# The weight sums of a wide pair's quarters on GpSimd instead of VectorE, in a three-layer attention and MoE kernel

## Chip, cores and metric

The kernel runs on one core of one Trainium2 chip. The metric is device microseconds of one execution. Three executions before the change took 1060.55, 1061.58 and 1061.87 us; their median, 1061.58 us, is the time before.

## What is computed

A chunked attention, then two dense layers with different activations, all in float32:

```python
def reference(**kwargs):
    attn_out = _attn_ref(...)              # (4, 8, 768, 64), chunks of 32 queries
    x = attn_out.transpose(0, 2, 1, 3).reshape(B * S, H * D)   # 3072 x 512
    x = _moe_ref(x, w_in, w_out, alpha)    # h = x @ w_in; g = max(h,0) + alpha*min(h,0); g @ w_out
    return _moe2_ref(x, w_in, w_out)       # g = h * tanh(softplus(h)); g @ w_out
```

`w_in` is 512 x 2048 and `w_out` 2048 x 512 in both layers.

## The kernel before

**Numbers and blocks.** Every float32 operand of a matmul is kept as a rounded high part and a low part (its rest), and a product is three matmuls: high by high, high by low, low by high. The 3072 rows are six blocks of 512. A layer's 2048 hidden units are 16 units of 128 (`NJ`), or 8 pairs (`NPAIR`).

**Stages.** Attention is woven into the first blocks of layer 1. Blocks 0 to 3 of layer 1 are done unit by unit (`gemm1` line 1069, `gemm2` line 1118). Blocks 4 and 5 are done together in the *wide stage* (`pair1`, products at line 1552, second matrix at line 1648). Layer 2 follows (lines 1227 and 1359).

**The wide stage.** A pair of units and two blocks make a 2 x 2 by 2 x 2 matrix product. It is done with seven products instead of eight, so it needs sums and differences of the quarters of the weights and of the inputs. `wide_x` makes those of the inputs once. `sums_of_w(p)` makes those of pair p's weights, one pair ahead of `pair1(p)`:

- it first undoes the split: for both units, high plus low part into the tile `tt` (128x512 each, two additions, line 1513);
- then four differences of quarters in place in `tt` (128x256, line 1523), all by VectorE;
- then ScalarE copies `tt` rounded into `to` (line 1524), and VectorE subtracts to get the low half (line 1526).

`tt` has one buffer (in the profile a `b` tile), so the additions of pair p+1 wait for line 1526 of pair p. `to` has two (the tiles `xh` and `xl` of an old ring). Products 3 to 6 of a pair read `to`; products 0 to 2 read the weights themselves.

**A pair's evacuations.** Product 3 starts bank B, product 0 bank A. ScalarE copies both out (line 1559). Then products 4 and 2 add on, product 5 goes to A again, product 6 to A, product 1 to B anew. Between them VectorE adds each bank to what was kept (`more`, line 1562: one operand in PSUM, one in SBUF): `e3` after product 2, `e2` after product 5, `e1` after product 1. Product 6 cannot start before `e2` has been read out of bank A, nor product 1 before `e3` has been read out of bank B. The activation (lines 1566, 1567, 1570) and a split (lines 1629, 1630) make operands for the second matrix. Its matmuls (lines 1118 and 1648, *pieces* of three) stand between the products.

**Other work on VectorE in this stage.** The weights of layer 2 are read, converted and split in background jobs (lines 341, 344, 383, 392), and blocks 2 and 3 end (lines 1082, 1092).

**What sets the order.** The program is written down as tasks (`Plan.add`: engine, planned cost, function, reads, writes). `Plan.run` computes for each task when it is due, from the planned costs backwards, and then walks forward in time, giving each engine the ready task that is due first. The instructions are issued in that order, fixed for each engine, and each engine runs its queue in order. So a planned cost (`d_(512)`, 0.6 us, for a 128x512 VectorE operation) also sets where all other instructions stand. The five engines are VectorE, ScalarE, TensorE, SyncE (which issues the DMAs), and GpSimd, which so far has only memsets, the identity and the sign of `alpha` at the start.

Of the kernel before, what the change touches and what calls it, by code (L numbers as in the profile page):

```python
# [51 lines left out]
class Pool:  # L52
# [5 lines left out]
    def add(self, make, after):  # L58
        self.free.append((make, list(after)))
# [130 lines left out]
def chunked_attention_moe_moe_kernel(  # L190
# [16 lines left out]
    nc = tc.nc  # L207
# [48 lines left out]
    def a_(n):  # L256
        return 0.1 + 0.83e-3 * n

    def d_(n, fast=False):
        return 0.066 + n / (1920.0 if fast else 960.0)  # L260
# [735 lines left out]
    pool, wpool = Pool(), Pool()  # L996
# [510 lines left out]
    def sums_of_w(p):  # L1507
        w = [weights[0, "i", 2 * p + n] for n in range(2)]
        tt, to = second["tt"].next(), wide["t"].next()
        for n in range(2):  # L1510
            add(
                "dve", d_(512),
                lambda n=n: nc.vector.tensor_add(
                    tt.t[:, (1 - n) * 512 : (2 - n) * 512], w[n].t[:, 0, :].bitcast(F32), w[n].t[:, 1, :].bitcast(F32)
                ),
                [w[n]], [(tt, n)],
            )

        def q(i):
            return tt.t[:, PLACE.index(i) * HB :][:, :HB]  # L1520

        for to_, x, y in ((3, 5, 3), (5, 4, 5), (4, 4, 3), (6, 6, 4)):
            add("dve", d_(HB), lambda to_=to_, x=x, y=y: nc.vector.tensor_sub(q(to_), q(x), q(y)), [], [tt])
        add("act", a_(1024), lambda: nc.scalar.copy(to.t[:, :1024], tt.t), [tt], [(to, "h")])
        add(
            "dve", d_(1024), lambda: nc.vector.tensor_sub(to.t[:, 1024:], tt.t, to.t[:, :1024].bitcast(F32)),
            [tt, (to, "h")], [(to, "l")],
        )
        return to
# [177 lines left out]
    for layer, blk, j in tiles:  # L1707
# [13 lines left out]
        n = BLOCKS[blk][1]  # L1721
# [37 lines left out]
    for layer, blk, j in pend:  # L1759
        reload1(j)  # L1760
        parts.extend((6, part) for part in gemm2_parts(layer, blk, j))
    tops = {0: sums_of_w(0)}
    for p in range(NPAIR):
        if p + 1 < NPAIR:
            tops[p + 1] = sums_of_w(p + 1)
        if p in JOBS_AT:
            next(jobs)(plan.now + 25.0)
        ends_ = pair1(p, xs, take)
        take(12)
        if p < NPAIR - 1:  # L1770
            for j in (2 * p + 1, 2 * p):
                parts.extend(wide_parts(WIDE, j, (p, j) == (0, 1), False))
# [108 lines left out]
```

## Time and profile before

| | before |
|---|---|
| median of three executions | 1061.58 us |
| the profiled execution | 1062.53 us |
| its span on the core | 1060.7 us |
| TensorE busy | 1053.6 us (99%) |
| VectorE busy | 769.7 us (73%) |
| ScalarE busy | 605.3 us (57%) |
| GpSimd busy | 6.7 us (1%) |
| mean granted TensorE clock | 0.998 |

The span lies 1.8 us below the execution's own time, which includes what stands around it. Busy shares are means over stages: VectorE's 73% is made of stretches of over 90% and others under 60%. Instructions of one engine overlap a little at their ends, so the time that one takes in a full queue is the distance between two starts, not its duration.

### The profile page before, as it was taken

The numbers are of one execution on the slowest core, as the hardware profiler recorded it, in microseconds if no ns is written. First come the engines' busy times: TensorE is split into PE (matmuls) and PEld (weight loads), VectorE is DVE, ScalarE is ACT, GpSimd is POOL, SyncE is SP. The second block draws the span as 40 slices with busy tenths as digits, with TensorE's granted clock in tenths as the row PEclk, the third lists the DMA queues.
The fourth block names the chain that finished last, engine by engine and source line by source line (L and its number), as shares of the span: only waits on it lengthen the run. The fifth ranks groups of instructions, "written<-read, shape, count | busy, mean of one in ns | idle before, by whom it ended". The sixth has DMA issues, their size and how long they took to land.

```text
span 1060.7 us, 22413 instructions
## 1 busy us (share of the span) xinstructions
PE 1053.6 (99%) x8249; PEld 905.6 (85%) x8249; DVE 769.7 (73%) x1626; ACT 605.3 (57%) x1505; POOL 6.7 (1%) x19
## 2 busy tenths in 40 slices
PE   9999999999999999999999999999999999999998
PEld 5888888888888888888888889999999999999998
DVE  6899487779877799999595246776576875475586
ACT  6888545565556555787585344654444654454453
POOL 2000000000000000000000000000000000000000
PEclk9999999999999999999999999999999999999999
DMA  9968783876577655577799898687888778778786
GB/s 275 301 218 232 258 282 108 236 243 210 198 235 229 213 179 195 169 254 255 242 303 334 283 304 265 218 259 251 263 271 252 227 245 250 229 239 253 229 267 203
DMA packets 136732, 256.68 MB, mean 242 GB/s; under 512 B 13872, under 2 KB 38960, under 8 KB 136624
## 3 DMA queue, kind: packets, MB, share of 16 engines
q1 hardware_dynamic: 136624, 255.26, 75.2%
q8 instruction: 65, 1.06, 0.4%
q14 instruction: 43, 0.35, 0.1%
HBM read 203.56 MB, written 51.64 MB: 241 GB/s over the span
## 4 chain that ended last, share of the span: by engine, by line
PE 99%; issue 0%; DVE 0%; DVEq 0%
PE bank L1359 23%; PE bank L1227 22%; PE bank L1118 17%; PE bank L1069 17%; PE bank L1648 8%; PE bank L1552 7%; PE bank L803 2%; PE bank L737 1%; PE bank L1666 1%; PE bank L681 0%; PE bank L614 0%; PE bank L850 0%; PE bank L874 0%; DVE xh L1420 0%; DVEq L1876 0%
## 5 line engine op out<-in xcount | busy, mean ns | idle before, releaser
L1227 PE MATMUL bank<-wi,wo 128*128 128x512 f32 x672 | 180.7, 392 | 0.0
L1069 PE MATMUL bank<-xh,wi 128*128 128x512 f32 (+1 forms) x528 | 170.9, 386 | 0.0
L1118 PE MATMUL bank<-gh,wo 128*128 128x512 f32 x512 | 170.2, 392 | 0.0
L1227 PEld LDWEIGHTS bank<-wi,wo 128*128 128x128 f32 x672 | 121.5, 189 | 21.3
L1069 PEld LDWEIGHTS bank<-xh,wi 128*128 128x128 f32 x528 | 98.2, 188 | 19.9
L1118 PEld LDWEIGHTS bank<-gh,wo 128*128 128x128 f32 x512 | 96.1, 188 | 20.6
L1069 PE MATMUL bank<-xl,wi 128*128 128x512 f32 (+1 forms) x264 | 101.1, 383 | 0.0
L1118 PE MATMUL bank<-gl,wo 128*128 128x512 f32 x256 | 99.7, 390 | 0.0
L1227 PE MATMUL bank<-wo,wo 128*128 128x512 f32 x336 | 93.0, 393 | 0.0
L1359 PE MATMUL bank<-wo,wi 128*128 128x256 f32 x588 | 80.2, 283 | 0.0
L1359 PEld LDWEIGHTS bank<-wo,wi 128*128 128x128 f32 x588 | 77.1, 191 | 3.0
L1359 PE MATMUL bank<-wo,wo 128*128 128x256 f32 x558 | 76.9, 283 | 0.0
L1359 PEld LDWEIGHTS bank<-wo,wo 128*128 128x128 f32 x558 | 73.7, 191 | 3.1
L1227 PEld LDWEIGHTS bank<-wo,wo 128*128 128x128 f32 x336 | 60.8, 189 | 10.1
L1088 ACT ACTIVATE rstrip<-bank 128x512 f32<-128x512 f32 x64 | 39.0, 609 | 47.1 <-PE bank L1069 45.3
L1081 ACT CAST gh<-rstrip 128x512 fp32r<-128x512 f32 x64 | 40.4, 632 | 44.3 <-PE bank L1118 22.6
L1092 DVE SCALAR_TENSOR_TENSOR rstrip<-rstrip,nalpha 128x512 f32<-128x512 f32 x64 | 47.8, 748 | 22.4 <-ACT rstrip L1089 21.6
L1069 PEld LDWEIGHTS bank<-xl,wi 128*128 128x128 f32 x264 | 49.6, 188 | 9.5
L891 DVE STREAM_TRANSPOSE aT<-s 32x256 f32<-32x256 f32 x128 | 55.8, 436 | 2.4
L1082 DVE TENSOR_TENSOR gl<-rstrip,gh 128x512 fp32r<-128x512 f32 x64 | 44.0, 688 | 18.1 <-ACT gh L1081 17.3
L1118 PEld LDWEIGHTS bank<-gl,wo 128*128 128x128 f32 x256 | 48.1, 188 | 9.7
L756 ACT ACTIVATE s<-bank,su 128x64 f32<-128x64 f32 x160 | 48.7, 351 | 7.5 <-DVE su L773 7.5
(399 smaller groups left out, 1999.3 us busy)
## 6 DMA issues: line engine op xcount, KB each, us to landing
wo<-w2o SPq DMA_DIRECT2D x237, 256.0 KB, 3.4
wo<-w2i SPq DMA_DIRECT2D x168, 256.0 KB, 3.4
wo<-w1o SPq DMA_DIRECT2D x49, 512.0 KB, 4.3
w2o<-wo SPq DMA_DIRECT2D x57, 256.0 KB, 3.1
w2i<-wo SPq DMA_DIRECT2D x56, 256.0 KB, 3.2
wo<-in_w_out_dram SPq DMA_DIRECT2D x24, 512.0 KB, 7.6
wi<-in_w_in_dram SPq DMA_DIRECT2D x16, 512.0 KB, 9.0
w1o<-wo SPq DMA_DIRECT2D x16, 512.0 KB, 5.6
```

The lines of the kernel that those rows point to most:

```text
L756: nc.scalar.activation(s()[:, i, z, g], ps(z)[:, i, g], AF.Exp, bias=st.t[:, 0, n : n + 1], scale=0.125, accum_out=st.t[:, 1, n : n + 1],)
L891: nc.vector.transpose(dst[:, :, m // 2, m % 2], src[:, :, keys])
L1069: nc.tensor.matmul(bk.t[:, lo:hi], a, b, start=kk == 0 and i == 0, stop=kk == KT - 1 and i == 2)
L1081: add("act", a_(n), lambda: nc.scalar.copy(g.t[0], src.t[0]), [src], [(g, "h")], at=at)
L1082: add("dve", d_(n), lambda: nc.vector.tensor_sub(g.t[1], src.t[0], g.t[0].bitcast(F32)), [src, (g, "h")], [(g, "l")], at=at)
L1088: add("act", a_(n) - 0.05, lambda: nc.scalar.activation(m.t[0], h.t[:, :n], AF.Relu, scale=-1.0), [h], [m], at=at)
L1092: lambda: nc.vector.scalar_tensor_tensor(r.t[0], m.t[0], nalpha[:, j : j + 1], r.t[0], ALU.mult, ALU.add),
L1118: nc.tensor.matmul(bk.t[:, :n], lt, rh, start=j == 0 and i == 0, stop=j == NJ - 1 and i == 2)
L1227: nc.tensor.matmul(bk.t, l, r, start=start and kk == n == 0, stop=kk == 1 and n == 2, skip_group_check=True,)
L1359: nc.tensor.matmul(bk.t[:, s * HB : (s + 1) * HB], g.t[:, zg * HB + s * P : zg * HB + (s + 1) * P], piece()[:, zw * HB : (zw + 1) * HB], s ...
L1552: nc.tensor.matmul(bk.t, l, r, start=start and kk == n == 0, stop=kk == 1 and n == 2, skip_group_check=True,)
L1648: nc.tensor.matmul(bk.t, lt, rh, start=first and i == 0, stop=last_ and i == 2)
```

## The change

The two additions of `sums_of_w` go from VectorE's queue to GpSimd's. The planner is told 1.2 us for one of them instead of 0.6 us, and places everything again.

```diff
@@ -1509,8 +1509,8 @@
         tt, to = second["tt"].next(), wide["t"].next()
         for n in range(2):
             add(
-                "dve", d_(512),
-                lambda n=n: nc.vector.tensor_add(
+                "pool", 1.2,
+                lambda n=n: nc.gpsimd.tensor_add(
                     tt.t[:, (1 - n) * 512 : (2 - n) * 512], w[n].t[:, 0, :].bitcast(F32), w[n].t[:, 1, :].bitcast(F32)
                 ),
                 [w[n]], [(tt, n)],
```

Three places show how the order moves; rows that are left out between two shown ones are marked. In the names, `b_4901` is the tile `tt` before; in the changed program `tt` is `b_4903`, and `b_4901` a tile of `wide_x`.

VectorE, where the sums of pair 0 begin (the difference, before to changed):

```order
 L1082 TENSOR_TENSOR gl<-rstrip,gh 128x512
-L1513 TENSOR_TENSOR b_4901<-wi_408 128x512
-L1513 TENSOR_TENSOR b_4901<-wi_429 128x512
+L1460 TENSOR_TENSOR b_4901<-wo_3703,wo_3704 128x1024
 L392 TENSOR_TENSOR wo_1906<-wf_4695,wo_1906 128x256
 L827 TENSOR_TENSOR xl_4498<-bank_4821,xh_4497 128x2x4x64
```

The two additions are gone from the queue; a 128x1024 addition of `wide_x`, which stood further back, takes their place.

VectorE, up to the weight sums' last step of pair 0 (line 1526), and from the last 128x1024 step of `wide_x` (line 1481) to the second bank that is read out (line 1562). Before:

```order
L1481 TENSOR_TENSOR wo_5065<-b_4957,wo_5030 128x1024
L1472 TENSOR_TENSOR b_5023<-b_4957,b_5023 128x1024
L1092 SCALAR_TENSOR_TENSOR rstrip<-rstrip,nalpha 128x512
L1460 TENSOR_TENSOR b_5088<-wo_3670,wo_3671 128x1024
L1526 TENSOR_TENSOR xh_5077<-b_4901,xh_5077 128x1024
...
L1481 TENSOR_TENSOR xl_4498<-b_5088,xh_4497 128x1024
L1513 TENSOR_TENSOR b_4901<-wi_505 128x512
L1513 TENSOR_TENSOR b_4901<-wi_557 128x512
L1523 TENSOR_TENSOR b_4901<-b_4901 128x256 x3
L1562 TENSOR_TENSOR b_4957<-bank_5105,b_4957 128x512
L1523 TENSOR_TENSOR b_4901<-b_4901 128x256
L1562 TENSOR_TENSOR b_4936<-bank_5090,b_4936 128x512
```

Changed:

```order
L1481 TENSOR_TENSOR wo_5052<-b_4959,wo_5019 128x1024
L1082 TENSOR_TENSOR gl<-rstrip,gh 128x512
L1472 TENSOR_TENSOR b_4901<-b_4959,b_4901 128x1024
L1460 TENSOR_TENSOR b_5073<-wo_3670,wo_3671 128x1024
L1092 SCALAR_TENSOR_TENSOR rstrip<-rstrip,nalpha 128x512
L392 TENSOR_TENSOR wo_1912<-wo_1912 128x256
L1526 TENSOR_TENSOR xh_5079<-b_4903,xh_5079 128x1024
...
L1481 TENSOR_TENSOR xl_4498<-b_5073,xh_4497 128x1024
L1523 TENSOR_TENSOR b_4903<-b_4903 128x256 x4
L1562 TENSOR_TENSOR b_4959<-bank_5106,b_4959 128x512
L1526 TENSOR_TENSOR xl_5164<-b_4903,xl_5164 128x1024
L1562 TENSOR_TENSOR b_4938<-bank_5093,b_4938 128x512
```

From the first addition to line 1526 of pair 0 the queue holds the same instructions as before, without the two additions and with one more 128x256 operation (line 392); the others only change places among themselves. All four differences of pair 1 now stand ahead of the first bank that is read out, and line 1526 of pair 1 ahead of the second.

TensorE, from product 0 to product 3 of pair 0. Before:

```order
L1552 MATMUL bank_5090<-wo_3703,wi_408 128x512
L1118 MATMUL bank_4223<-gh,wo_5000 128x512
L1118 MATMUL bank_4223<-gl,wo_5000 128x512
L1118 MATMUL bank_4223<-gh,wo_5000 128x512
L1552 MATMUL bank_5105<-wo_5030,xh_5077 128x512
```

Changed:

```order
L1552 MATMUL bank_5093<-wo_3703,wi_408 128x512
L1552 MATMUL bank_5106<-wo_5019,xh_5079 128x512
L1552 MATMUL bank_5106<-wo_5052,xh_5079 128x512
L1552 MATMUL bank_5106<-wo_5019,xh_5079 128x512 x2
L1552 MATMUL bank_5106<-wo_5052,xh_5079 128x512
L1552 MATMUL bank_5106<-wo_5019,xh_5079 128x512
L1118 MATMUL bank_4223<-gh,wo_5002 128x512
```

The piece of the second matrix that stood between the two products comes behind product 3. A second piece that stood ahead of product 4 moves back too; of the two, one then stands between products 5 and 1 and one behind product 6.

## Rows read from the trace of the kernel before

**Rows 1.** The page, part 1: busy time, share, instructions of each engine.

```profile
PE 1053.6 (99%) x8249; PEld 905.6 (85%) x8249; DVE 769.7 (73%) x1626; ACT 605.3 (57%) x1505; POOL 6.7 (1%) x19
```

**Rows 2.** All waits of TensorE (line waited, for what: us in total, times, longest).

```profile
PE bank L1666 <- issue: 1.4, 1, 1.4
PE bank L1666 <- DVE busy L1664: 1.2, 1, 1.2
PE bank L737 <- PE bank L1069: 0.2, 1, 0.2
```

**Rows 3.** VectorE in stretches: us, busy (instructions), PEclk, DMA share, GB/s.

```profile
391.00:507.00 116.00, 113.49 (x211) 1.00 0.68 224
427.00:507.00 80.00, 78.66 (x156) 1.00 0.72 238
```

**Rows 4.** VectorE, 391 to 507 us, groups by line: the additions, and reads of banks.

```profile
L1562 DVE TENSOR_TENSOR b<-bank,b 128x512 f32<-128x512 f32 x18 | 12.2, 680 | 0.8 <-PE bank L1552 0.8
L1513 DVE TENSOR_TENSOR b<-wi 128x512 f32<-128x512 f32 x16 | 10.6, 682 | 0.4 <-PE bank L803 0.4
L266 DVE COPY rstrip<-bank 128x512 f32<-128x512 f32 x2 | 1.4, 683 | 0.0
L827 DVE TENSOR_TENSOR xl<-bank,xh 128x512 fp32r<-128x512 f32 x2 | 1.4, 681 | 0.0
```

**Rows 5.** Timeline of GpSimd and VectorE, first 8 us (start, duration).

```profile
1.21 0.29 POOL masks.py:199 TENSOR_SCALAR_AFFINE_SELECT ident<-ident 128x128 f32<-128x128 f32 x1
2.96 0.52 POOL L475 MEMSET qbd<- 64x512 f32 x1
3.25 0.51 DVE L266 COPY qbd<-wo 64x512 f32<-64x512 f32 x1 [2.13 <-DMA wo<-in_q_dram]
5.37 0.52 POOL L475 MEMSET wo<- 64x512 f32 x1
5.52 0.65 DVE L266 COPY qbd<-wo 64x512 f32<-64x512 f32 x1 [1.75 <-DMA wo<-in_q_dram]
5.95 0.69 POOL L475 MEMSET wi<- 64x512 f32 x1
6.59 0.42 DVE L266 COPY qbd<-wo 64x512 f32<-64x512 f32 x1
7.85 0.41 DVE L266 COPY wo<-wi 64x512 f32<-64x512 f32 x1
```

**Rows 6.** Line 475: durations in ns (min/median/max), first and last start.

```profile
L475 POOL MEMSET wi<- x2: 689/740/792, 5.9 to 6.7; 64x512 f32 x2
```

**Rows 7.** Timeline of VectorE around the sums of pairs 0 and 1.

```profile
391.25 1.29 DVE L1513 TENSOR_TENSOR b<-wi 128x512 f32<-128x512 f32 x2 [0.45 <-PE bank L803]
392.46 0.42 DVE L392 TENSOR_TENSOR wo<-wf,wo 128x256 fp32r<-128x256 f32 x1
...
413.81 1.21 DVE L1526 TENSOR_TENSOR xh<-b,xh 128x1024 fp32r<-128x1024 f32 x1
414.94 0.67 DVE L1082 TENSOR_TENSOR gl<-rstrip,gh 128x512 fp32r<-128x512 f32 x1
...
424.00 0.68 DVE L1562 TENSOR_TENSOR b<-bank,b 128x512 f32<-128x512 f32 x1
424.60 0.42 DVE L1523 TENSOR_TENSOR b<-b 128x256 f32<-128x256 f32 x1
424.93 0.69 DVE L1562 TENSOR_TENSOR b<-bank,b 128x512 f32<-128x512 f32 x1
```

**Rows 8.** Timeline of TensorE in the same stretch: products and pieces of pair 0.

```profile
412.99 1.52 PE L1552 MATMUL bank<-wo,wi 128*128 128x512 f32 x6
414.35 0.39 PE L1118 MATMUL bank<-gh,wo 128*128 128x512 f32 x1
...
415.02 1.52 PE L1552 MATMUL bank<-wo,xh 128*128 128x512 f32 x6
...
423.19 1.52 PE L1552 MATMUL bank<-wo,xh 128*128 128x512 f32 x6
424.74 1.66 PE L1552 MATMUL bank<-wo,wi 128*128 128x512 f32 x6
426.23 0.39 PE L1552 MATMUL bank<-xh,xh 128*128 128x512 f32 x1
```

**Rows 9.** Product 6 of pair 3: TensorE, and VectorE's read of the bank.

```profile
468.57 0.68 DVE L1562 TENSOR_TENSOR b<-bank,b 128x512 f32<-128x512 f32 x1
468.93 0.39 PE L1648 MATMUL bank<-gh,wo 128*128 128x512 f32 x1
469.30 0.50 PE L1552 MATMUL bank<-xh,xl 128*128 128x512 f32 x1
```

## Prediction

> **What bounds the kernel now.** I read the busy times first, then the waits of TensorE, then VectorE by stretches, then the timelines of both around the sums. TensorE is busy for 99% of the span [rows 1], and all its listed waits are 2.8 us, none of them in the wide stage [rows 2]. So work taken from another engine gains next to nothing by itself. The stage has a second limit, though. From 391 to 507 us VectorE is busy for 113.49 of 116 us [rows 3]. It keeps up with TensorE, but barely. Pair 0 shows it: line 1526 starts at 413.81 and is done by 414.94, when the next instruction starts [rows 7]; product 3, which reads its result, starts at 415.02 [rows 8]. Product 1 of this pair starts at 424.74, where six matmuls from 423.19, 1.36 us apart like 412.99 and 414.35, would have ended at 424.55: it waited 0.19 us for the bank that VectorE was reading out from 424.00 [rows 7, 8]. Product 6 waited another 0.13 us (426.23 against 424.74 + 1.36). Product 6 of pair 3 starts at 469.30, 0.37 us behind the matmul before it where 0.23 us is the step (1.36 over six): it waited 0.14 us for a read that began at 468.57 [rows 9]. These seams come to 0.46 us; with a few more like the last one I put what could be won there at 0.6 us.
>
> **Removed.** 16 additions leave VectorE's queue, 10.6 us busy [rows 4]. In the full queue one costs 0.60 us: two from 391.25 to 392.46 [rows 7]. That is 16 x 0.60 = 9.7 us.
>
> **Added.** GpSimd gets the 16 additions. Nothing stands behind them in its queue. The trace has no addition on GpSimd, so I bound one. Below: a memset of 512 elements, 0.52 us, which only writes. A select that reads and writes 128 elements takes 0.29 us, so four times that, 1.18 us, for 512 [rows 5]. Above: a second operand read as dearly as the first, 1.18 + (1.18 - 0.52) = 1.84 us. I take 1.2 us, by the nearest row, the one that reads too; its fixed part, counted four times, stands in for the second operand. The Trainium skill (GPSIMD Engine Reference, Performance versus the Vector engine) gives 4497 ns for an addition of 2048 elements, by which I estimate 1.12 us for 512; the sum below would then be +3.0 instead of +4.1 us. No run here shows it yet.
>
> **Do the engines hold each other?** At the start of the trace GpSimd memsets and VectorE copies overlap, and the one that starts second is longer. The copy at 5.52 takes 0.65 us where a lone one takes 0.41: a memset had begun at 5.37 and ran 0.37 us into it. The memset at 5.95 takes 0.69 where others take 0.52: the copy ended 0.22 us into it. The next memset (the last start, 5.95 + 0.69 = 6.64 at the earliest) takes 0.79, and a copy ran until 7.01 [rows 5, 6]. The lengthening, 0.24, 0.17 and 0.27 us, is the overlap less about 0.1 us. So I take that a VectorE instruction that meets an addition on GpSimd waits 1.2 - 0.1 = 1.1 us. Which ones meet? Those that read a bank use PSUM for one operand, and I count them as free: 12.2 + 1.4 + 1.4 = 15.0 us of the 113.49 - 10.6 us that stay [rows 3, 4]. 85% are left, and the **hold** is 0.85 x 1.1 = 0.94 us per addition. That is more than the 0.60 us that each takes off VectorE. These rows show memsets and copies, not additions with two operands: that is the largest guess here.
> The Trainium skill (SBUF — State Buffer, Who interferes with whom) says that VectorE and GpSimd share a port pair as an exclusive lock, that a VectorE instruction with two SBUF inputs blocks against a GpSimd instruction that reads SBUF, and that one with a single SBUF input does not. By it the hold is the whole 1.2 us, 1.02 us per addition, and the sum +5.4 us. It speaks against this change; nothing in this trace shows the two-input case.
>
> **The sum at the front (pairs 0 and 1).** VectorE has no idle time to give here.
> - Line 1526 of pair 0: done at 414.94 - 1.21 (two additions gone) + 0.33 (a line 392 now ahead; 424.60 to 424.93 is one such step [rows 7]) + 2 x 0.94 = 415.94. TensorE's new order has product 3 right behind product 0, at 414.35 [rows 8]. Wait: 1.59 us.
> - The read-out of `e3`: started 424.00, now 424.00 - 2.42 + 0.33 (a fourth line 1523 ahead) + 4 x 0.94 = 425.67, done 0.60 later, 426.27. TensorE comes to product 1 at 424.55 - 2 x 0.68 + 0.68 (two pieces go behind, one comes back ahead; a piece is three steps) + 1.59 = 425.46. Wait: 0.81 us.
> - The read-out of `e2` now stands behind line 1526 of pair 1: 426.27 + 1.13 + 0.60 = 428.00; product 6 could start at 426.27 + 1.36 = 427.63. Wait: 0.37 us.
> Together 2.77, less the 0.19 + 0.13 us waited there before: **+2.45 us**. TensorE has no idle time later in which to regain it.
>
> **The sum of the rest (12 additions).** VectorE's queue grows by 12 x (0.94 - 0.60) = 4.1 us. From this go its idle time from 427 to 507, 80 - 78.66 = 1.3 us [rows 3], and the 1.1 us by which TensorE is now later (2.45) than VectorE (4 x 0.94 - 2.42 = 1.34). The seam of rows 9 leaves no other slack. **+1.7 us.** Behind 507 VectorE has idle time again, and nothing more is lost. The moved DMA issues (SyncE's queue shifts by a few places) and ScalarE's shifts I cost at nothing: both follow VectorE, and ScalarE is busy for 57% [rows 1]. If ScalarE's cast between lines 1523 and 1526 no longer fits, the front grows by up to a cast's half microsecond.
> In all +4.1 us on the profiled 1062.53, 1066.7 us. The median of the runs is 0.95 us below that execution, so I forecast **1065.7 us**.
> Bounds: an addition of 0.52 us gives a hold of 0.36 us; then the front has a wait of 0.4 us, no more than it loses now, and up to 0.6 us of the seams is won: 1061.0 to 1061.7. One of 1.84 us gives 1.48 us of hold: +4.6 at the front, +8.2 after it, 1074.4 us. For my own case, holds of 0.8 to 1.2 us, the same working gives 1063.7 to 1069.9.
>
> **Rivals.**
> 1. *No hold* (not slower). Two-operand additions on VectorE might not meet GpSimd's at all, or the holds might fall into VectorE's waits. It turns at a hold of about 0.75 us, where the working above gives +1.7 us. Below that the 9.7 us off VectorE win the seams: 1061.2 us. For it: only memsets and copies are seen to collide. Against it: each overlap seen cost time to the later one.
> 2. *GpSimd kept out.* A full VectorE queue may hold off the addition until VectorE itself stops at line 1523, which waits for it. Then each pair costs two additions in the open, 2.4 us, less 1.2 us off the queue: 8 x 1.2 - 1.3 = +8.3, 1069.9 us; at 1.84 us an addition 8 x 2.5 - 1.3 = +18.7, 1080 us. For it: one `tt` buffer, so an addition cannot start earlier than line 1526 of the pair before, and ahead of pair 3's differences only one instruction stands between. Against it: three to seven instructions stand there in most pairs.
> 3. *Faster by more than the seams.* A freer VectorE lets the planner order TensorE more tightly. It would need over 2 us, and no row shows a wait that large after the start.
>
> **Chances.** A measurement of this kernel tells about 0.2%, 2.1 us, from no change. My case 0.50, rival 1 0.38, rival 2 0.07, rival 3 0.05. A hundredth of my case falls short of 1063.7 us. So slower 0.49 + 0.07 = 0.56, same 0.38 + 0.01 = 0.39, faster 0.05. The range goes from 1060.9, which takes in nearly all of rival 1, to 1070.0, the top of my case and the first price of rival 2; about 0.14 is left outside.
>
> **What would show it.** Right: GpSimd's 16 rows of line 1513 near 1.2 us; VectorE instructions with two SBUF operands longer than before beside them, and those that read banks not; product 3 of pair 0 waiting over 1 us for line 1526. VectorE busy 391 to 507 should rise despite 16 instructions fewer. Wrong: VectorE's durations unchanged and TensorE without waits (rival 1); additions of several us and VectorE idle before line 1523 (rival 2); or the time going to a place outside the wide stage.

## The result, and the profile after

The changed kernel takes **1073.1 us** (median of 4 runs, 1070.96 to 1073.43) against 1061.1 us for the kernel before on the same chip (4 runs, 1059.78 to 1061.87): a ratio of **1.0104**, 95% interval 1.0088 to 1.0121. It is slower, as forecast, but by 12.0 us, not by 4.1, and the time lies above the range. The profiled execution took 1072.83 us, its span is 1071.0 us.

The page's busy times (part 1 of the kernel after) answer to [rows 1]: 16 instructions went from VectorE to GpSimd, and nothing got shorter. VectorE is busy for 2.0 us *longer* with 16 instructions fewer.

```profile
PE 1056.0 (99%) x8249; PEld 905.5 (85%) x8249; DVE 771.7 (72%) x1610; ACT 605.4 (57%) x1505; POOL 36.9 (3%) x35
```

TensorE's waits of the kernel after (line waited, for what: us in total, times, longest) answer to [rows 2]. The wide stage, line 1552, had no entry there; now it has two, on VectorE's read-outs (line 1562) and on `xh` (line 1526).

```profile
PE bank L1552 <- DVE b L1562: 7.1, 5, 2.5
...
PE bank L1552 <- DVE xh L1526: 0.8, 1, 0.8
```

The wait list counts a stand only where it is long enough to be named. So I also took TensorE's idle time from its timeline: the distance of two starts less 0.227 us for each matmul between them (six take 1.36 us). From 391 to 545 us that is 0.9 us before and 12.8 us after, 11.9 us more, so nearly all of the loss lies in this stage. The spans differ by 10.3 us only, because the profiled execution of before lost some 2.5 us at its start (TensorE's granted clock was 0.84 and 0.82 from 15 to 25 us). The changed kernel is therefore 2.4 to 2.5 us ahead when the stage begins: its first two additions start at 388.83 us, those of before at 391.25 [rows 7].

**The additions on GpSimd.** The durations of line 1513 (ns: shortest, median, longest), then GpSimd's timeline (start, duration, line, in brackets the idle time before and its releaser); a row with x2 spans both additions of a pair:

```profile
L1513 POOL TENSOR_TENSOR b<-wi x16: 1274/1579/7229, 388.8 to 499.1; 128x512 f32<-128x512 f32 x16
```

```profile
388.83 3.71 POOL L1513 TENSOR_TENSOR b<-wi 128x512 f32<-128x512 f32 x2 [379.36 <-PE bank L803]
413.28 8.47 POOL L1513 TENSOR_TENSOR b<-wi 128x512 f32<-128x512 f32 x2 [20.73 <-DVE xh L1526]
426.07 2.98 POOL L1513 TENSOR_TENSOR b<-wi 128x512 f32<-128x512 f32 x2 [4.31 <-DVE xl L1526]
436.49 2.54 POOL L1513 TENSOR_TENSOR b<-wi 128x512 f32<-128x512 f32 x2 [7.44 <-DVE xh L1526]
```

A pair takes 2.54 us where nothing disturbs it, 1.27 us an addition. One pair, that of pair 1 at 413.28, takes 8.47 us, and its first addition alone 7.23.

**VectorE is held.** Groups of VectorE from 391 to 507 us in the kernel after (instructions | busy us, mean ns of one | idle before):

```profile
L1570 DVE SCALAR_TENSOR_TENSOR b<-rstrip,nalpha,b 128x512 f32<-128x512 f32 x14 | 12.1, 867 | 0.9 <-ACT b L1567 0.6
L1562 DVE TENSOR_TENSOR b<-bank,b 128x512 f32<-128x512 f32 x17 | 11.6, 682 | 1.6 <-PE bank L1552 1.6
L392 DVE TENSOR_TENSOR wo<-wf,wo 128x256 fp32r<-128x256 f32 x15 | 10.6, 718 | 0.9 <-ACT wo L389 0.9
...
L341 DVE TENSOR_SCALAR wf<-raw 128x512 uint32<-128x512 uint32 x5 | 4.3, 856 | 0.0
```

The groups of lines 1570, 392 and 341 before:

```profile
L1570 DVE SCALAR_TENSOR_TENSOR b<-rstrip,nalpha,b 128x512 f32<-128x512 f32 x16 | 11.8, 743 | 0.1
L392 DVE TENSOR_TENSOR wo<-wf,wo 128x256 fp32r<-128x256 f32 x18 | 7.2, 413 | 0.0
L341 DVE TENSOR_SCALAR wf<-raw 128x512 uint32<-128x512 uint32 x5 | 2.1, 417 | 0.0
```

Line 1562, which reads a bank, stands at 682 ns against 680 [rows 4]. The means rise because single instructions are up to 1.1 us longer while GpSimd adds: line 392 takes 1.51 us at 389.87 and 1.52 at 497.95, line 341 takes 1.52 us at 448.07. I call the sum of such lengthenings over the stage (each group's count times its mean, less its mean before) the **hold**. It is 9.9 us, 0.62 per addition. Counted the other way, by single instructions that are over 0.1 us longer, it is 9.8 us, on eleven instructions, seven of them 1.0 to 1.1 us longer. In the runs below the two counts differ by up to 0.7 us.

**VectorE also stands.** From 391 to 507 us VectorE was busy for 113.49 us before [rows 3] and is busy for less after (the same columns):

```profile
391.00:507.00 116.00, 108.07 (x465) 86.19 (x463) 105.76 (x181) 73.49 (x137) 28.21 (x16) 1.00 0.62 204
```

For the same piece of work the stretch has to end at the same event. I take it from the first additions to the start of product 6 of pair 5, the last place where TensorE stands: 391.0 to 499.5 us before, 388.6 to 507.4 after. One row of each kernel:

```profile
391.00:499.50 108.50, 108.47 (x487) 88.73 (x479) 105.99 (x196) 75.08 (x142) 0.00 (x0) 1.00 0.67 219
```

```profile
388.60:507.40 118.80, 110.47 (x478) 88.17 (x474) 108.43 (x183) 75.52 (x141) 30.37 (x16) 1.00 0.62 203
```

The stretch is 10.3 us longer: VectorE is busy 2.4 us longer (third pair of numbers) and idle 7.9 us longer (118.80 - 108.43 = 10.4 against 2.5). Its waits in this stretch of the kernel after say for what:

```profile
DVE b L1523 <- POOL b L1513: 3.6, 2, 2.4
DVE b L1562 <- PE bank L1552: 1.6, 2, 0.8
DVE wi L1570 <- ACT wi L1567: 1.1, 2, 0.6
DVE wo L392 <- ACT wo L389: 0.9, 2, 0.7
```

3.6 us are for GpSimd's additions. The others, 6.3 us with those not shown (before: 2.2 us in all), are for TensorE and ScalarE, which themselves come later.

**Two places in detail.** At the front, VectorE's timeline around pair 1's additions:

```profile
413.12 0.41 DVE L392 TENSOR_TENSOR wo<-wf,wo 128x256 fp32r<-128x256 f32 x1
...
418.14 1.21 DVE L1481 TENSOR_TENSOR xl<-b,xh 128x1024 fp32r<-128x1024 f32 x1
421.79 1.80 DVE L1523 TENSOR_TENSOR b<-b 128x256 f32<-128x256 f32 x4 [2.44 <-POOL b L1513]
```

From 413.12 to 419.35 VectorE runs eight instructions back to back, lines 392, 1082, 1472 and 1481, each with two operands in SBUF and each at its usual length. The addition released at 413.28 ends only at 413.28 + 7.23 = 420.51, 1.2 us (its own length) after that queue has run dry. Then line 1523 stands for 2.44 us. TensorE, 388 to 430 us of the kernel after, pays behind it at products 1 and 6, and before it at product 3 (from its third matmul on, the first that reads line 1526's low half):

```profile
411.82 0.61 PE L1552 MATMUL bank<-wo,xh 128*128 128x512 f32 x2
413.26 1.19 PE L1552 MATMUL bank<-wo,xh 128*128 128x512 f32 x4 [0.82 <-DVE xh L1526]
...
424.25 1.66 PE L1552 MATMUL bank<-wo,wi 128*128 128x512 f32 x6 [1.15 <-DVE b L1562]
426.64 0.50 PE L1552 MATMUL bank<-xh,xh 128*128 128x512 f32 x1 [0.73 <-DVE b L1562]
```

At pair 5, VectorE between line 1526 and the read-out that product 6 needs:

```profile
496.20 1.22 DVE L1526 TENSOR_TENSOR xh<-b,xh 128x1024 fp32r<-128x1024 f32 x1 [0.16 <-ACT xh L1524]
497.35 0.68 DVE L1630 TENSOR_TENSOR gl<-b,gh 128x512 fp32r<-128x512 f32 x1
497.95 1.52 DVE L392 TENSOR_TENSOR wo<-wf,wo 128x256 fp32r<-128x256 f32 x1
499.39 1.78 DVE L1570 SCALAR_TENSOR_TENSOR wi<-rstrip,nalpha,wi 128x512 f32<-128x512 f32 x1
...
506.71 0.68 DVE L1562 TENSOR_TENSOR b<-bank,b 128x512 f32<-128x512 f32 x1
```

The same two before:

```profile
491.92 1.23 DVE L1526 TENSOR_TENSOR xh<-b,xh 128x1024 fp32r<-128x1024 f32 x1 [0.19 <-ACT xh L1524]
...
498.75 0.68 DVE L1562 TENSOR_TENSOR b<-bank,b 128x512 f32<-128x512 f32 x1
```

There the read-out starts 6.83 us behind line 1526; now it is 10.51 us. The 3.7 us are: two additions gone, -1.2; two holds (lines 392 and 1570), +2.1; and 2.6 us of other work (lines 1630, 1570, two of 1523, two of 392) that stood elsewhere in the order before and now stands between. TensorE waits 2.54 us for it, and then its granted clock is 0.50, 1.2 of 2.4 GHz, over the next 2.5 us (windows of the kernel after; the seventh number is the clock):

```profile
505.00:507.50 2.50, 0.06 (x1) 0.06 (x1) 2.50 (x8) 1.64 (x5) 0.00 (x0) 0.97 0.55 205
507.50:510.00 2.50, 2.50 (x6) 2.04 (x7) 2.47 (x6) 1.58 (x3) 0.00 (x0) 0.50 0.63 234
```

The matmuls from 507.44 to 511.84 us take some 1.4 us longer for that in this execution.

### The profile page after: what moved, and what is told of

Its sections match the earlier page's. It is cut to its first block, busy times and chain, and to the rows that moved or that the text cites. A ratio compares the mean times of both kernels' runs of the same rounds, so it can differ in the third digit from the quotient of the medians.

```text
span 1071.0 us, 22430 instructions
## 1 busy us (share of the span) xinstructions
PE 1056.0 (99%) x8249; PEld 905.5 (85%) x8249; DVE 771.7 (72%) x1610; ACT 605.4 (57%) x1505; POOL 36.9 (3%) x35
## 4 chain that ended last, share of the span: by engine, by line
PE 88%; DVE 6%; issue 2%; ACT 1%; DMA 1%; POOL 1%; SPq 0%; DVEq 0%; ACTq 0%
PE bank L1359 22%; PE bank L1227 21%; PE bank L1069 15%; PE bank L1118 15%; PE bank L1648 6%; PE bank L1552 3%; PE bank L803 2%; PE bank L737 1%; POOL b L1513 1%; DVE wo L392 1%; PE bank L1666 1%; DVE b L1523 1%; DVE wo L383 1%; DVE wf L341 1%; DVE b L1570 1%
```

## The experiments

All are timed against the kernel before on the same chip (its medians: 1061.34 us for the first four, 1061.1 for the next four, 1061.24 for the last four). Theory H: VectorE and GpSimd hold each other. W: the cost is VectorE's wait at line 1523. O: the cost is the new order of the work. Above are the results, below the runs one by one.

| run | us (lowest to highest) | ratio, interval |
|---|---|---|
| the change | 1073.11 (1070.96 to 1073.43) | 1.0104, 1.0088 to 1.0121 |
| e1 new order, additions on VectorE | 1065.71 (1065.25 to 1065.85) | 1.0037, 1.0024 to 1.0051 |
| e2 old order, additions on GpSimd | 1068.90 (1067.39 to 1069.63) | 1.0065, 1.0050 to 1.0080 |
| e3 before + 16 unused additions | 1078.02 (1076.82 to 1081.68) | 1.0159, 1.0139 to 1.0179 |
| e4 before + 32 unused memsets | 1061.97 (1061.10 to 1065.65) | 1.0005, 0.9993 to 1.0017 |
| e5 the change, memsets for additions | 1061.46 (1060.44 to 1064.77) | 1.0006, 0.9995 to 1.0017 |
| e6 the change without pair 1 | 1070.23 (1070.06 to 1070.81) | 1.0083, 1.0068 to 1.0098 |
| e7 the change, two `tt` tiles | 1072.31 (1071.32 to 1072.45) | 1.0100, 1.0085 to 1.0115 |
| e8 the change, planned at 3.0 us | 1071.55 (1070.41 to 1072.59) | 1.0094, 1.0079 to 1.0109 |
| e9 old order, pairs 2 to 7 on GpSimd | 1066.48 (1064.68 to 1069.11) | 1.0050, 1.0037 to 1.0062 |
| e10 new order, pairs 2 to 7 on GpSimd | 1069.38 (1068.59 to 1070.57) | 1.0079, 1.0067 to 1.0091 |
| e11 before + 12 unused additions | 1075.96 (1072.68 to 1077.17) | 1.0133, 1.0117 to 1.0150 |
| e12 before + 16 unused copies | 1065.43 (1065.15 to 1067.06) | 1.0044, 1.0030 to 1.0059 |

**e1 and e2: the order and the engine apart.** e1 plans the additions as GpSimd's and gives them to VectorE; e2 does the reverse.

```
e1   the change:        nc.gpsimd.tensor_add(   ->  nc.vector.tensor_add(
e2   the kernel before: nc.vector.tensor_add(   ->  nc.gpsimd.tensor_add(
```

> The changed program's order on every engine, but the sixteen additions issued by VectorE again, at the places that the planner gave them on GpSimd. Theory H (a GpSimd addition and a VectorE instruction with two SBUF operands shut each other out) and theory W (VectorE's queue stands at line 1523 because GpSimd is late): both need GpSimd, so the time is that of before within 0.3%, 1058 to 1065 us. Theory O (the new order leaves the seams of TensorE without cover, whoever adds): at least half of the loss of 12 us is there, 1067 us or more.

> The order of before on every engine, only the sixteen additions leave VectorE's queue for GpSimd's. H: collisions as in the changed kernel, 1067 us or more, with single VectorE instructions of line 392, 1570 or 341 about 1.1 us longer beside an addition. W: VectorE waits for GpSimd at line 1523 in nearly every pair, since there the differences follow closely on the additions: 1068 to 1085 us, and the waits at line 1523 sum to over 8 us. O: 1060 to 1063 us.

e1 gave 1065.7 us, between what H and W and what O expected: the new order costs 4.4 us while VectorE still does the additions. e2 gave 1068.9 us, 7.6 more than before in the old order. That is H's time, and W falls: only one wait at line 1523, 2.4 us, not over 8. The two losses, 4.4 and 7.6, add up to the change's 12.0 us, but they are not two separate causes: e5 below has the new order and loses nothing.

**e3 and e4: GpSimd's work alone.** Into the kernel before, behind each line 1526, I put work on GpSimd that no one uses: in e3 two additions that read the low half of `to`, in e4 one small multiply that does (so that they start at the same place) and four memsets. Nothing leaves VectorE.

```
         for n in range(2):                                             # e3
+            add("pool", 1.2, lambda n=n: nc.gpsimd.tensor_add(spare_.t,
+                to.t[:, 1024:1536].bitcast(F32), to.t[:, 1536:].bitcast(F32)), [(to, "l")], [spare_])
```
```
+        add("pool", 0.3, lambda: nc.gpsimd.tensor_scalar_mul(spare_.t[:, :16],       # e4
+            to.t[:, 1024:1040].bitcast(F32), 1.0), [(to, "l")], [spare_])
+        for n in range(4): add("pool", 0.6, lambda n=n: nc.gpsimd.memset(spare_.t, 0.0), [], [spare_])
```

> The kernel before, unchanged on all other engines, and beside it two 128x512 additions on GpSimd after each line 1526 that read the finished low half and write a tile nobody reads. Nobody waits for them. H: VectorE keeps its sixteen additions and is shut out up to sixteen times for up to 1.1 us: 1066 to 1080 us. W and O: nothing waits and no order changed: 1059 to 1063 us.

> As with the spare additions, but after each line 1526 GpSimd does one small multiplication that reads the same tile (128x16, to begin at the same time) and then four memsets of 128x512 that only write. If only reading on GpSimd collides with two-operand VectorE instructions: 1059 to 1063 us, with at most the few single-operand VectorE instructions (line 341) longer. If any GpSimd access shuts VectorE out: eight times 2.1 us of memset beside a full queue, 1066 us or more.

e3: 1078.0 us, a hold of 13.2 us; some 3 us of the loss come from two stretches at a granted clock of 0.51 and 0.52, behind stands of 3.0 and 3.1 us. e4: 1062.0 us, no difference, a hold of 0.7 us, which lies on two instructions of line 341 (one operand), 0.4 us each. So it is GpSimd's *reading* that costs, with nothing waiting for it and no order changed; W and O fall as the main cause. e4's small multiply shows the shut-out once more, at the place of the 7.23 us addition, and again at 476.58 us. GpSimd in e4, and one line of VectorE (line 1562 is line 1568 here):

```profile
413.31 7.72 POOL L1531 TENSOR_SCALAR spare<-xh 128x16 f32<-128x16 f32 x1 [404.31 <-DVE xh L1526]
...
436.87 0.26 POOL L1531 TENSOR_SCALAR spare<-xh 128x16 f32<-128x16 f32 x1 [7.28 <-DVE xh L1526]
...
445.60 0.56 POOL L1531 TENSOR_SCALAR spare<-xl 128x16 f32<-128x16 f32 x1 [6.13 <-DVE xl L1526]
...
476.58 3.64 POOL L1531 TENSOR_SCALAR spare<-xl 128x16 f32<-128x16 f32 x1 [12.70 <-DVE xl L1526]
...
480.03 0.68 DVE L1568 TENSOR_TENSOR b<-bank,b 128x512 f32<-128x512 f32 x1
```

The same instruction takes 0.26 us elsewhere, so for 7.5 us it did not work, it was kept out. At 476.58 VectorE runs seven instructions back to back, two of them line 341 with its one operand; the eighth, at 480.03, reads a bank, and the multiply ends 0.19 us into it. In e11 and e12 the GpSimd instruction shut out at this place also ends within its own length of the start of that bank read (1.24 us into it for an addition, 0.55 for a copy).

**e5: the change without the reading.** Each addition of the change becomes two memsets on GpSimd; the sums are left out of the computation.

```
-                lambda n=n: nc.gpsimd.tensor_add(
+                lambda n=n: [nc.gpsimd.memset(tt.t[:, (1 - n) * 512 : (2 - n) * 512], 0.5) for _ in range(2)],
```

> The changed kernel with its order kept on all other engines, but each addition on GpSimd replaced by two memsets of the same 128x512 half of the sums' tile, about 1.1 us together, which read nothing. The sums of the two parts are left out (the tile holds a constant). H, with only reads colliding: VectorE is rid of sixteen additions and never shut out, so 1057 to 1063 us. W or O (a wait for GpSimd, or the new order, does the harm): 1066 us or more.

1061.5 us, the time of the kernel before. Order, engine, place and dependences are the change's; the reading is gone, and with it 11.7 us and all but 0.5 of the 3.6 us for which line 1523 waited. It also prices the other side. VectorE's 16 additions are gone here as well, VectorE is idle for 8.7 of 108.4 us (the same stretch), and nothing is won:

```profile
388.60:497.00 108.40, 107.96 (x483) 88.79 (x475) 99.68 (x183) 75.72 (x142) 15.73 (x32) 1.00 0.67 220
```

**e6, e7 and e8: can the wait at line 1523 be had out of the way?** e6 leaves pair 1's additions, the ones kept out, on VectorE; e7 gives `tt` a second tile, so that the additions may start a pair earlier; e8 plans an addition at 3.0 us, so that its result is awaited later.

```
e6   *(("dve", d_(512)) if p == 1 else ("pool", 1.2)),  (nc.vector if p == 1 else nc.gpsimd).tensor_add(
e7   second["tt"] = Ring([*wholes[4:], late([P, 1024], "b5")]); second["tt"].last = [att_bufs, att_bufs]
e8   "pool", 1.2,  ->  "pool", 3.0,
```

> As the changed kernel, but the two additions of pair 1 stay with VectorE; in the changed kernel GpSimd was kept out there for 7.2 us and VectorE then stood 2.4 us at line 1523. If that stand is a cost of its own: 1.5 to 4 us less than the changed kernel, 1069 to 1071.5 us. If only the sum of the holds counts: an eighth of 12 us less, 1071.5 us or more.

> As the changed kernel, with two tiles for the sums instead of one, so that the additions of a pair need not wait for line 1526 of the pair before and lie a pair ahead of the differences. W: the stand at line 1523 goes and with it most of the loss, 1061 to 1064 us. H: the sixteen collisions stay, 1066 to 1073 us, with no wait for GpSimd left.

> As the changed kernel, but the planner is told 3.0 us for an addition instead of 1.2, so that it places the differences further behind. W: 1061 to 1064 us. H: holds stay, the waits at line 1523 go, 1065 to 1072 us.

e6 takes 2.9 us off and has no wait at line 1523: pair 1's two additions cost about what the stand was (2.4 us). The intervals of e6 and the change overlap (1.0068 to 1.0098, 1.0088 to 1.0121), so the size is rough; the slowest of e6's executions lies below the fastest of the change's. e7 and e8 give 1072.3 and 1071.6 us, within H's times and far from W's. Neither got rid of the wait: in e7 line 1523 waits three times, 4.2 us in all; in e8 once, 2.4 us.

**e9 to e11: the 12 additions of pairs 2 to 7 alone.** The part that the prediction calls the rest cost far more than its 1.7 us, and the runs so far don't say why; these three take it alone. e9 is e2 and e10 is the change, both with pairs 0 and 1 on VectorE; e11 is e3 with 12 unused additions, where those of pairs 2 to 7 start.

```
e9   (nc.vector if p < 2 else nc.gpsimd).tensor_add(        # planned as VectorE's, as before
e10  *(("dve", d_(512)) if p < 2 else ("pool", 1.2)),  (nc.vector if p < 2 else nc.gpsimd).tensor_add(
e11  for n in range(2 if 1 <= p <= 6 else 0):
```

> The order of before on every engine, the additions of pairs 0 and 1 left on VectorE, the 12 of pairs 2 to 7 on GpSimd. Theory F (the 0.6 us that each addition frees on VectorE pays for most of its hold, as long as the order leaves it free; the planned order spends it on work pulled ahead): 1062 to 1065.5 us, near the +1.7 us that the prediction gave to these 12. Theory G (freed time pays for nothing in any order, every hold shows whole): 12 x 0.62 = 7.4 us above the kernel before, 1067 to 1071 us. Theory K (nearly all of the loss comes from pairs 0 and 1): 1060.5 to 1062.5 us.

> Additions of pairs 0 and 1 on VectorE in the plan and in fact, those of pairs 2 to 7 on GpSimd, planned at 1.2 us, so that the order is a new one. Theory F: 1067 to 1071 us, over 2 us slower than the same 12 additions in the old order. Theory G: 1067 to 1071 us, and the same 12 in the old order no faster. Theory K: 1060.5 to 1063 us.

> The kernel before, all its own additions on VectorE, and 12 further additions on GpSimd that nobody uses, started where those of pairs 2 to 7 would start. No time is freed. Theories F and G: 12 holds of 0.6 to 0.9 us show, 1068 to 1073 us. Theory K: under 1064 us.

K falls: these 12 cost 5.2 us in the old order, 8.1 in the new one and 14.7 with no time freed. e11 lies above the 1073 us that F and G allowed; its profiled execution, at 1072.7, lies within. e9 lies between F's times and G's, so freed time pays for a part of the hold only. e10 is where both had it, but 2.9 us above e9, and the two intervals do not meet: that speaks for F, the order spends what is freed. Some 1.5 of the 2.9 us arise at half the clock: e10's profiled execution has a granted clock of 0.50 behind a stand of 2.6 us, longer than any in e9, and e9's shows none.

```profile
489.30:492.40 3.10, 3.10 (x8) 2.40 (x8) 2.58 (x5) 2.42 (x6) 0.00 (x0) 0.50 0.70 204
```

One row each for e9 and e11, the same stretch as above:

```profile
388.60:502.20 113.60, 109.28 (x494) 88.69 (x486) 109.43 (x184) 74.60 (x142) 19.07 (x12) 1.00 0.64 210
```

```profile
388.60:508.70 120.10, 110.35 (x494) 88.46 (x486) 117.77 (x197) 74.96 (x142) 21.70 (x12) 1.00 0.61 202
```

In e11 VectorE gets 11.8 us busier (a hold of 11.2, 0.93 for each addition) and the stretch 11.6 us longer: every hold lands on TensorE. In e9 the hold is 9.4 us (0.78 each; 10.1 counted by the twelve instructions that are longer) and 7.2 us are freed; the stretch is still 5.1 us longer, 3.4 of it busy time of VectorE and 1.7 idle time. 6.0 us of this hold fall on six instructions of line 341, which reads a single operand. Its groups in e9's stretch (before: means of 418 and 417 ns):

```profile
L341 DVE TENSOR_SCALAR wf<-wo 128x512 uint32<-128x512 uint32 x5 | 5.4, 1073 | 0.0
L341 DVE TENSOR_SCALAR wf<-raw 128x512 uint32<-128x512 uint32 x5 | 4.8, 967 | 0.4 <-ACT raw L338 0.4
```

TensorE does not lose at every pair that is held. Beside the additions of the six pairs VectorE is held for 1.5, 0.5, 1.9, 2.1, 1.9 and 2.1 us; up to the next pair's additions TensorE loses 1.3, 0.0, 0.1, 1.9, 0.2 and 2.0 us. The fourth, at pair 3's products, shows how, with VectorE's instructions in the order of before:

```profile
461.99 1.79 DVE L1570 SCALAR_TENSOR_TENSOR wi<-rstrip,nalpha,wi 128x512 f32<-128x512 f32 x1
463.70 1.51 DVE L341 TENSOR_SCALAR wf<-raw 128x512 uint32<-128x512 uint32 x1
...
469.29 0.68 DVE L1562 TENSOR_TENSOR b<-bank,b 128x512 f32<-128x512 f32 x1
```

Lines 1570 and 341 are 1.05 and 1.09 us longer than before (0.74 and 0.42), two additions of 0.60 us are gone, so the read-out comes 0.94 us later after line 1526. TensorE stands 1.8 us for it where it lost 0.14 us before [rows 9]. Another 0.7 us of that line 1526 had brought along: it starts 2.1 us later in the stage than before, and TensorE had lost only 1.4 us more by then.

**e12: does one operand do?** e3 with copies in place of the additions.

```
-                lambda n=n: nc.gpsimd.tensor_add(spare_.t,
-                    to.t[:, 1024:1536].bitcast(F32), to.t[:, 1536:].bitcast(F32))
+                lambda n=n: nc.gpsimd.tensor_copy(spare_.t, to.t[:, 1024:1536].bitcast(F32))
```

> The kernel before and 16 copies on GpSimd that nobody uses (one operand read, 128x512), at the places where 16 further additions gave 1078.0 us and pure writes 1062.0 us. If any read of SBUF by GpSimd holds VectorE's two-operand instructions: the loss goes by the copies' duration, 1068 to 1076 us. If only two-operand reads do: 1060 to 1063 us.

Between the two: 1065.4 us, a hold of 3.8 us (0.24 for each copy; the shortest copy takes 0.61 us, the median is 0.95). A single read collides too, and is shut out at the same place (8.85 us for two). Eleven VectorE instructions are longer, none by more than 0.42 us. That is 0.2 us less than the shortest copy, as the 1.1 us of the additions are 0.2 us less than 1.27: a hold goes by the length of the GpSimd instruction that is met.

## Why the prediction was right or wrong

**TensorE bounds the stage, and work taken from VectorE gains next to nothing: right.** e5 frees VectorE of all 16 additions and gains nothing (ratio 1.0006). The seams I put at 0.6 us are below what can be measured.

**An addition on GpSimd, 1.2 us: right.** 1.27 us undisturbed. The estimate from the Trainium skill (GPSIMD Engine Reference, Performance versus the Vector engine), 1.12 us, is 12% short of it.

**The hold: right in kind and for one instruction, in part by luck.** I took 1.1 us for an instruction that meets an addition: the rows show 1.0 to 1.1 for seven of the eleven that are held. I took 0.94 us for each addition: e11 has 0.93, e9 0.78, the change 0.62. Bank reads are not held: line 827 at 391.31 takes 0.68 us beside an addition, as before [rows 4]. So the mechanism I called the largest guess held. But the rows I took it from show memsets beside single-operand copies. By e4 memsets lengthen no two-operand instruction, only line 341, and that by at most 0.41 us; that the same rule, overlap less 0.1 us, fits additions beside two-operand instructions was luck. So is the fit of 0.94 to e11: it is an average by share of the queue, and the change, in which eleven instructions are held, does not keep to it. The trace agrees with the Trainium skill (SBUF — State Buffer, Who interferes with whom) that VectorE instructions with two SBUF inputs collide with a GpSimd instruction that reads, and not with one that only writes (e3 against e4). My shorter form of it, that one with a single SBUF input does not, was too wide: line 341 is held (1.52 against 0.42 us), for 2.2 of the 9.8 us in the change and 6.0 of the 10.1 in e9. The same section excepts the two-port modes from its rule and says that a `tensor_scalar`, which line 341 is, can run in one; I had left that out.

**The front, +2.45 us: 3.7 us.** TensorE's idle time up to product 6 of pair 0 is 4.0 us, less the 0.3 of before. Product 3 stood 1.0 us (forecast 1.59), product 1 1.3 (0.81), product 6 0.9 (0.37); the rest is 0.4 us at product 4, forecast at nothing, and 0.1 us behind each stand. At product 3 I had not used that its first two matmuls read only the high half: they run at 411.82, in time, and save 0.45 us. The misses at products 1 and 6 come behind the 2.44 us stand at line 1523, which is rival 2 at one of its eight places. I had weighed it against "three to seven instructions" between, and not asked whether those instructions read two SBUF operands; here all do. e6 prices it at roughly 2.9 us.

**The rest, "12 x (0.94 - 0.60)" less idle time, +1.7 us: 8.2 us. This is the step that failed.** Not by the hold, which was smaller than I took it, but by setting freed time off against it. The runs show three parts:
- With nothing freed, a hold lands whole on TensorE (e11: hold 11.2, stretch +11.6 us). The idle time of VectorE that I set off, 1.3 us, absorbed next to nothing: VectorE is idle for 2.3 us of the stretch in e11, and was for 2.5 before.
- With time freed in the same order (e9: 7.2 us), 9.4 us of hold still cost 5.1 us. The additions start as line 1526 ends. At three of the six pairs the held instructions stand ahead of what TensorE waits for next (pair 3 above), and it loses 1.3 to 2.0 us there; at the other three it loses 0.2 us or less. The time freed in between does not come back to TensorE: VectorE is idle 1.7 us longer. That it becomes idle because VectorE then waits for TensorE's later product is argued from the waits, not tested.
- In the planned order freed time is not left at all: other work is drawn forward into it. With the additions back on VectorE, that order has 2.4 us more VectorE work in the stretch (108.36 us in e1 against 105.99) and costs 4.4 us. With the time really free (e5) it costs nothing. With the time taken back by holds it costs about the same again: e10 is 2.9 us slower than e9, the change loses 12.0 us where e2 loses 7.6. Part of this is the clock, 1.4 to 1.5 us in the profiled executions of e10 and the change, behind stands that are longer than those of the old order (by the starts of the matmuls 2.6 and 2.7 us, against 1.9 in e9 and e2).

Of the 8.2 us, 1.4 us are at half the clock behind the longest stand, a term that I did not have. For the whole stage VectorE's books read: 2.4 us drawn forward, 9.6 freed, 9.9 held, together +2.7 (measured +2.4); and 7.9 us more idle, 3.6 of it waiting for GpSimd. Two small slips changed nothing: by its own working the bottom of my case is 1063.5 us, not 1063.7; and the 0.13 us that I put ahead of product 6 of pair 0 were lost inside product 1, whose six matmuls take 1.66 us where others take 1.52 [rows 8].

**What was to show it.** Product 3 waits for line 1526, but 0.8 us, not over 1. "VectorE busy 391 to 507 should rise" was wrong: it fell to 105.76 us, since I had not foreseen that VectorE would itself wait. Rival 1 (no hold) is out by e3. Rival 3 (faster) is out by e5: with the reads of SBUF gone altogether the time is that of the kernel before, so in this order even additions that hold nothing would not beat it measurably, and none of the runs did; other orders were not tried in that way.

What stays open: a bank read lets a shut-out GpSimd instruction in (e4, e11, e12 above), but what shuts it out is not settled. In the change the addition at 497.51 gets in behind one two-operand instruction, that at 413.28 behind none of eight; in e4 the multiply meets the same two instructions, a line 1630 and a line 1513, at 445.60 and at 476.58, and gets in behind the first of them in one case only. And e9's executions spread from 1064.7 to 1069.1 us, which one profile does not explain.

## What to carry to other kernels

Moving work from a busy VectorE to GpSimd frees VectorE only of what it is not made to wait for in return: compare the time freed with the holds, on instructions that read two SBUF operands and on single-operand ones like line 341 too, and look at what stands right behind the place where GpSimd starts. Do not set time freed in one place off against time lost in another when two engines wait for each other in turn; follow the one read-out that the bounding engine waits for. And where the order is planned from costs, a cost that leaves out such holds makes the planner spend time that does not exist; before moving work at all, replace it once by something that reads nothing (as e5 does), to see what the move could win at best.

## What was not expected of the hardware

- **A shut-out, not just a hold.** Behind a VectorE queue of eight two-operand instructions an addition of 1.27 us took 7.23 us; behind one of eleven, in e4, a multiply of 16 columns took 7.72 us in place of 0.26. VectorE's instructions kept their length, so in that stretch GpSimd alone paid. A bank read of VectorE ended such a shut-out (e4, at 480.03 us).
- **One operand does not protect.** Beside additions line 341, with one operand, is lengthened by up to 1.1 us, as much as two-operand instructions, and it alone is lengthened beside memsets too (by up to 0.41 us).
- **A hold is some 0.2 us shorter than the GpSimd instruction.** An addition of 1.27 us (median 1.58) lengthens one instruction by up to 1.1 us; a copy of 0.61 us (median 0.95) by up to 0.42 us.
- **The clock after a stand.** TensorE's granted clock fell to 0.50 behind the stand of 2.54 us at 504.9 us. In e11, behind a stand of 2.92 us at 505.8 us, the profiled execution kept 1.00; it is the fastest of its four at 1072.7 us, and the other three show mean clocks of 0.996 to 0.997 and take 2.2 to 4.5 us longer.
